# A planner's instruction orders and engine choices replaced in a fused attention and channel-mix kernel

## The chip, the cores and the metric

The kernel runs on one core of a Trainium2 chip. Times are microseconds (us) on the device; lower is better. The kernel before has a median of 170.34 us over 13 runs (169.53 to 171.25). The engines are PE (TensorE), VectorE (DVE in the profile), ScalarE (ACT), GpSimd (POOL) and SyncE (SP), which here only issues DMAs.

## What is computed

Attention with a sink of 4 keys and a window of 128, in 4 batches of 8 heads with 768 positions of 64 elements, and behind it a channel mix with a token shift:

```python
scores = np.where(is_sink | in_window, scale * q @ k.T, -1e9)
a = exp(scores - max); a = a / sum(a)
x = (a @ v).transpose(0, 2, 1, 3).reshape(B, S, H * D)      # [4, 768, 512]
xk = mu_k * x + (1 - mu_k) * x_prev                          # x_prev: x of the token before
xr = mu_r * x + (1 - mu_r) * x_prev
k = np.maximum(xk @ w_k, 0)                                  # w_k 512 x 1024
out = sigmoid(xr @ w_r) * ((k * k) @ w_v)                    # w_r 512 x 512, w_v 1024 x 512
```

All inputs and the output are float32; the kernel multiplies in bf16.

## The kernel before

The sequence is cut into 12 tiles of 256 tokens (u = 0 to 11: three for each of four batches; T = u % 3). For each tile:

- `load`: q, k and v of the tile, each 512 KB, go from HBM to the buffers `qs`, `ks`, `vs` (three of each), in one DMA or in two halves of 256 KB, all of them on SP's queue.
- `prepare`: casts to bf16 (`kb`, `qb`, `vb`), then a transpose to `kt` and `qt`. For k of tiles 4 to 11 and q of tiles 8 to 11 the transpose is a DMA on SP's queue (L608); for the others it is done on PE (`prep`, L621) and copied out of PSUM (L629).
- `attend`: scores `sc` for two pairs of heads at a time (L706), exp to `e` (L742, ScalarE), the mask (L756, VectorE), the product with v in `o` (L768 and L780), reciprocal and scaling to `x` (L793, L796).
- `mix`: transpose of x on PE (`xtp`, L819), copy to `xt` (L828), the token shift: `td` (L846) and four `xk` and four `xr` (L857).
- `ffn`: `kp` = xk @ w_k (L907), relu to `rl` (L917, L921), square to `kk` (L930, L934), `rp` = xr @ w_r (L946), tanh to `th` (L952), `vp` = kk @ w_v (L964), the gate in `ob` (L973; three `ob` buffers), and the store to HBM on SP's queue (L980).

The weights come as five loads of 1 MB (`wk` in two, `wr`, `wv` in two) and are cast once.

Every one of these steps is recorded as a numbered operation by `P.op` of the class `Plan`; the number is the place in the order of recording. `CHOICE` maps a number to an engine for operations that more than one engine can do. `ORDER` holds, for each engine, the numbers in the order in which it runs them. `Plan.schedule` merges the five lists into one program: it takes, again and again, the head of the list that its own model of durations lets start first, gives it the buffers of a pool that come free first by that model, and, where PE would be idle by that model in the first 32 us, puts in fills (L984: products with a tile of zeros, into a free bank). Constants of that model are the `service` of a DMA and the additions to the landing time in `schedule`. They are used for nothing else than the merge, the buffers and the number of fills. Each engine takes its instructions in order; an instruction that waits holds those behind it.

Numbers that are spoken of later: 0 to 66 are the loads. Of tile 7's, 8's, 9's, 10's, 11's loads: k is 38/39, 43/44, 49/50, 55/56, 61/62; q is 40, 45/46, 51/52, 57/58, 63/64; v is 41/42, 47/48, 53/54, 59/60, 65/66. The DMA transposes of tile 9 are 729, 731, 733, 735, of tile 10 806 to 812 (even), of tile 11 882 to 888 (even). The first scores of tiles 2, 9, 10 and 11 are 236, 783, 859 and 935. Stores: 470 and 466 of tile 3 (their `ob` is 469 and 465), 551 and 547 of tile 4, 627 and 623 of tile 5 (626, 622), 699 and 703 of tile 6 (698, 702).

Of the kernel before, what the change touches and what calls it, by code (L numbers as in the profile page):

```python
# [18 lines left out]
    83: "ACT", 87: "ACT", 89: "ACT", 93: "DVE", 96: "DVE", 97: "POOL", 99: "DVE", 102:  # L19
    "DVE", 103: "ACT", 104: "ACT", 128: "DVE", 134: "DVE", 137: "DVE", 140: "DVE", 141:  # L20
    "DVE", 150: "DVE", 178: "DVE", 181: "DVE", 187: "DVE", 190: "ACT", 191: "DVE", 200:
    "DVE", 208: "DVE", 209: "ACT", 261: "DVE", 270: "DVE", 271: "DVE", 276: "DVE", 300:
    "ACT", 341: "DVE", 344: "DVE", 346: "DVE", 350: "ACT", 352: "DVE", 359: "DVE", 368:
    "ACT", 372: "ACT", 376: "ACT", 417: "DVE", 421: "DVE", 427: "ACT", 428: "DVE", 437:
    "DVE", 446: "ACT", 454: "ACT", 458: "ACT", 495: "POOL", 499: "DVE", 500: "DVE", 502:
    "DVE", 505: "DVE", 506: "ACT", 511: "DVE", 518: "DVE", 527: "ACT", 531: "ACT", 535:
    "ACT", 539: "ACT", 574: "DVE", 579: "DVE", 581: "POOL", 584: "ACT", 585: "ACT", 607:
    "ACT", 656: "DVE", 660: "DVE", 661: "ACT", 663: "DVE", 670: "DVE", 679: "ACT", 683:
    "ACT", 691: "ACT", 734: "POOL", 736: "ACT", 737: "DVE", 742: "DVE", 749: "DVE", 758:
    "ACT", 761: "DVE", 766: "ACT", 770: "ACT", 813: "ACT", 814: "ACT", 823: "DVE", 832:  # L30
    "ACT", 839: "DVE", 840: "ACT", 844: "ACT", 883: "DVE", 885: "POOL", 889: "ACT", 890:
    "DVE", 899: "DVE", 908: "ACT", 912: "ACT", 915: "DVE", 920: "ACT", 958: "DVE", 974:
    "ACT", 982: "ACT", 1010: "ACT", 1014: "ACT",
# [24 lines left out]
        92, 95, 108, 109, 101, 79, 98, 118, 119, 115, 106, 111, 125, 121, 132, 158, 142,  # L58
        149, 129, 138, 135, 159, 156, 182, 188, 168, 169, 206, 234, 207, 161, 165, 175,
        171, 210, 192, 211, 199, 218, 219, 214, 179, 215, 185, 236, 289, 297, 301, 293,  # L60
        290, 298, 302, 294, 247, 239, 222, 224, 244, 250, 305, 230, 226, 255, 275, 227,
        259, 282, 231, 265, 309, 262, 310, 268, 317, 365, 307, 366, 342, 313, 328, 347,
        314, 373, 320, 374, 369, 325, 370, 336, 395, 377, 331, 351, 378, 383, 358, 381,
        393, 406, 385, 420, 386, 451, 273, 443, 452, 444, 389, 398, 425, 473, 403, 409,
        414, 390, 429, 447, 455, 436, 448, 456, 461, 471, 484, 459, 467, 498, 524, 536,
        525, 537, 503, 468, 528, 476, 529, 487, 552, 492, 508, 532, 481, 533, 463, 577,
        517, 510, 464, 563, 542, 555, 548, 540, 560, 549, 582, 630, 600, 586, 608, 601,
        566, 609, 544, 604, 571, 545, 605, 612, 593, 613, 641, 628, 616, 618, 633, 676,
        638, 677, 688, 680, 689, 681, 662, 704, 706, 649, 644, 684, 624, 685, 669, 620,
        625, 692, 621, 717, 709, 714, 694, 759, 755, 760, 756, 700, 741, 763, 739, 764,  # L70
        701, 767, 696, 725, 697, 768, 720, 783, 771, 773, 748, 779, 791, 775, 786, 780,
        794, 776, 815, 829, 837, 830, 833, 838, 834, 841, 857, 859, 802, 845, 797, 842,
        849, 822, 870, 853, 847, 862, 854, 905, 867, 906, 850, 909, 891, 910, 917, 913,
        878, 918, 923, 873, 921, 914, 935, 898, 929, 925, 933, 946, 930, 971, 979, 972,
        975, 980, 976, 938, 926, 954, 949, 943, 987, 983, 957, 984, 964, 989, 995, 991,
        996, 992, 999, 1003, 1000, 1004, 1007, 1011, 1008, 1012, 1019, 1015, 1017, 1020,
# [3 lines left out]
        69, 93, 96, 70, 102, 99, 80, 112, 113, 107, 116, 126, 137, 127, 122, 117, 123,  # L80
        128, 134, 150, 144, 147, 181, 145, 151, 152, 187, 146, 155, 153, 82, 81, 154, 148,
        140, 141, 208, 162, 163, 166, 176, 167, 172, 177, 173, 84, 194, 200, 195, 178,
        201, 196, 203, 202, 197, 221, 204, 85, 238, 213, 243, 191, 86, 217, 198, 240, 205,
        241, 249, 88, 245, 251, 246, 292, 252, 254, 90, 304, 256, 276, 257, 296, 277, 228,
        278, 261, 280, 284, 279, 285, 286, 232, 311, 341, 287, 344, 346, 319, 324, 281,
        270, 288, 271, 315, 335, 321, 326, 322, 330, 337, 327, 338, 417, 332, 352, 333,
        353, 397, 359, 354, 360, 356, 380, 361, 355, 362, 421, 387, 274, 364, 402, 413,
        399, 408, 400, 357, 404, 410, 405, 415, 411, 416, 391, 363, 431, 437, 434, 438,
        432, 450, 500, 439, 440, 433, 502, 442, 480, 499, 428, 486, 475, 491, 469, 477,
        478, 488, 505, 489, 435, 493, 509, 482, 494, 483, 574, 554, 441, 579, 511, 518,  # L90
        512, 559, 513, 519, 465, 556, 514, 557, 520, 561, 521, 562, 515, 565, 550, 523,
        632, 567, 516, 570, 522, 588, 568, 572, 573, 589, 637, 546, 590, 595, 591, 596,
        597, 656, 599, 634, 603, 635, 639, 643, 640, 611, 648, 663, 615, 592, 650, 645,
        651, 646, 660, 664, 665, 670, 598, 671, 708, 672, 626, 713, 666, 673, 710, 711,
        622, 715, 719, 716, 667, 724, 761, 687, 668, 742, 740, 743, 744, 746, 674, 675,
        726, 727, 702, 721, 722, 698, 762, 745, 737, 790, 749, 785, 750, 754, 792, 752,
        787, 747, 788, 751, 793, 781, 777, 801, 817, 818, 753, 839, 796, 836, 819, 803,
        804, 798, 820, 799, 821, 883, 823, 824, 861, 866, 826, 825, 863, 864, 855, 827,
        868, 877, 869, 851, 828, 893, 872, 879, 880, 894, 895, 874, 875, 896, 915, 899,
        900, 916, 904, 942, 901, 902, 937, 931, 948, 890, 897, 903, 953, 939, 940, 927,  # L100
        955, 950, 956, 944, 945, 951, 958, 978, 959, 962, 960, 986, 966, 963, 961, 967,
        968, 993, 997, 969, 970, 1002, 1006, 1021, 1029, 1025,
    ),
    "ACT": (
        67, 68, 91, 94, 100, 110, 114, 103, 104, 120, 124, 131, 133, 143, 130, 136, 139,
        160, 164, 183, 189, 157, 170, 174, 235, 209, 193, 83, 212, 184, 220, 180, 216,
        186, 237, 242, 190, 291, 299, 303, 248, 295, 223, 87, 253, 306, 225, 89, 258, 300,
        264, 260, 283, 267, 266, 263, 339, 269, 323, 318, 308, 367, 343, 334, 348, 329,
        375, 376, 371, 368, 396, 401, 372, 379, 419, 382, 394, 422, 384, 424, 412, 407,
        350, 445, 453, 426, 446, 474, 479, 430, 454, 427, 449, 457, 472, 462, 497, 460,  # L110
        485, 458, 490, 526, 538, 504, 530, 527, 553, 576, 558, 534, 531, 578, 535, 506,
        539, 543, 569, 564, 652, 541, 583, 631, 587, 602, 610, 654, 636, 658, 584, 606,
        594, 614, 585, 629, 617, 642, 619, 647, 678, 690, 705, 682, 607, 679, 707, 683,
        712, 691, 661, 728, 686, 730, 693, 718, 723, 732, 695, 757, 736, 765, 807, 766,
        758, 805, 769, 789, 772, 784, 774, 770, 811, 809, 795, 800, 816, 831, 835, 832,
        858, 860, 865, 846, 813, 843, 814, 840, 844, 848, 881, 876, 871, 907, 887, 892,
        911, 919, 912, 924, 908, 920, 941, 936, 889, 934, 922, 947, 952, 973, 977, 981,
        974, 982, 988, 985, 965, 990, 1001, 1005, 1009, 1013, 1014, 1010, 1016, 1018,
    ),
    "POOL": (  # L120
        73, 71, 78, 72, 76, 97, 75, 74, 77, 105, 272, 349, 495, 507, 581, 734, 738, 885,
    ),
    "SP": (
        0, 1, 3, 2, 4, 5, 7, 6, 16, 8, 10, 11, 9, 15, 12, 17, 18, 13, 14, 19, 20, 23, 25,
        24, 21, 22, 229, 340, 345, 28, 30, 29, 26, 233, 27, 418, 423, 312, 33, 31, 34, 35,
        392, 32, 496, 501, 36, 40, 38, 39, 37, 316, 575, 43, 580, 470, 45, 46, 388, 41,
        42, 44, 653, 655, 47, 659, 657, 49, 48, 551, 547, 51, 52, 53, 50, 731, 57, 735,
        729, 55, 627, 733, 623, 54, 466, 58, 56, 808, 699, 806, 812, 810, 63, 59, 60, 61,
        62, 782, 778, 64, 884, 882, 856, 886, 888, 703, 65, 66, 852, 932, 998, 928, 994,
        1022, 1030, 1026,  # L130
    ),
}


class Plan:

# [27 lines left out]
    def schedule(self):  # L164
# [37 lines left out]
        clock, port, dma, flying, mode = dict(BEGIN), {}, 0.0, [], 0  # L202
# [834 lines left out]
```

## Time and profile before

| | |
|---|---|
| median of 13 runs | 170.34 us (169.53 to 171.25) |
| the profiled execution, own time | 170.34 us |
| its span | 167.9 us |
| granted TensorE clock | 1.00 |
| HBM read, written | 24.12 MB, 6.29 MB |
| DMA packets | 81,762, of them 63,688 under 512 B |
| 256 KB load of k, v, q, from issue to landing (median) | 4.6, 4.6, 4.2 us |
| 1 MB load of a weight | 9.0 us |
| DMA transpose of k, q | 2.7, 3.2 us |
| store of 256 KB | 3.6 us |

The profile covers one execution. A group's row gives line, engine, operation, tiles, the count, then the engine's busy time and the mean of one, then the engine's idle time just before and what ended it. The chain of waits follows the work that ended last back to the start: each piece has its start, its length, and what it was.

### The profile page before, as it was taken

The page shows a single profiled execution, that of the slowest core. Times are in us where ns is not written, and L with a number is a line of the kernel's source. Part 1 is how long each engine was busy: PE and PEld are TensorE (multiplying, and loading weights), DVE is VectorE, ACT ScalarE, POOL GpSimd, SP SyncE. Part 2 cuts the span into 40 slices and gives each one's busy share as a digit, 9 for nine tenths or more (in the row PEclk, how much of TensorE's full clock was granted, in tenths as well). Part 3 has the DMA queues.
Part 4 walks back from the last instruction along what each step waited for, and adds up shares of the span by engine and source line. Part 5 has one row for each costly group of instructions (what it writes and reads, how often), then busy time and mean ns, then how long its engine had stood idle before and what let it go on. Part 6 is the DMA issues. An engine that isn't in the chain of part 4 may idle for free.

```text
span 167.9 us, 4234 instructions
## 1 busy us (share of the span) xinstructions
PE 160.8 (96%) x1627; PEld 105.0 (63%) x1627; DVE 145.0 (86%) x378; ACT 136.2 (81%) x223; POOL 12.7 (8%) x41
## 2 busy tenths in 40 slices
PE   7988999999999999999999999999989999999991
PEld 2445477855567586676576875766565685774850
DVE  2759999998999999999999889989988998988611
ACT  3777969999999999889899999768758978863450
POOL 7630000000100200100000001010000100000000
PEclk9999999999999999999999999999999999999999
DMA  4999999999879899997796797969979959100403
GB/s 138 246 294 331 206 359 301 282 358 274 198 179 270 188 215 257 158 265 164 188 275 137 166 290 173 158 162 264 202 77 234 286 129 246 67 4 0 168 19 125
DMA packets 81762, 33.81 MB, mean 201 GB/s; under 512 B 63688, under 2 KB 76240, under 8 KB 81744
## 3 DMA queue, kind: packets, MB, share of 16 engines
q1 hardware_dynamic: 81728, 33.56, 83.0%
q8 instruction: 12, 0.20, 0.5%
q14 instruction: 6, 0.05, 0.1%
q10 hardware_dynamic: 16, 0.00, 0.0%
HBM read 24.12 MB, written 6.29 MB: 181 GB/s over the span
## 4 chain that ended last, share of the span: by engine, by line
PE 65%; DVE 17%; DMA 12%; ACT 2%; issue 2%; SPq 0%
PE bank L907 17%; PE bank L964 15%; PE bank L946 9%; DMA qs<-in_q_dram 7%; PE sc L706 5%; PE bank L780 5%; PE bank L984 4%; DVE xk L857 3%; DMA kt<-kb 3%; DVE ob L973 2%; PE bank L621 2%; DVE x L796 2%; PE bank L819 2%; DMA out_dram<-ob 2%; PE bank L768 2%
## 5 line engine op out<-in xcount | busy, mean ns | idle before, releaser
L907 PE MATMUL bank<-xk,wk_sb 128*128 128x256 bf16 x384 | 50.2, 273 | 0.2 <-DVE wk_sb L563 0.2
L964 PE MATMUL bank<-wv_h,kk 128*128 128x512 bf16 x184 | 46.3, 379 | 0.0
L742 ACT ACTIVATE e<-sc 128x1024 bf16<-128x1024 f32 (+1 forms) x48 | 44.3, 964 | 1.7 <-PE sc L706 1.5
L907 PEld LDWEIGHTS <-wk_sb 128*128 128x128 bf16 x384 | 35.6, 98 | 8.5 <-DVE wk_sb L563 0.4
L917 ACT ACTIVATE rl<-bank 128x512 bf16<-128x512 f32 x44 | 25.9, 613 | 11.9 <-PE bank L907 10.0
L964 PEld LDWEIGHTS <-kk 128*128 128x128 bf16 x184 | 16.5, 98 | 14.3 <-DVE x L796 0.3
L756 DVE TENSOR_TENSOR e<-e,mask 128x1024 bf16<-128x1024 bf16 (+1 forms) x40 | 25.2, 641 | 0.1
L946 PE MATMUL bank<-wr_sb,xr 128*128 128x512 bf16 x96 | 24.0, 379 | 0.0
L857 DVE SCALAR_TENSOR_TENSOR xr<-td,mu_all,xt 128x256 bf16<-128x256 bf16 x48 | 22.7, 481 | 0.1
L857 DVE SCALAR_TENSOR_TENSOR xk<-td,mu_all,xt 128x256 bf16<-128x256 bf16 x48 | 22.0, 484 | 0.1
L973 DVE SCALAR_TENSOR_TENSOR ob<-th,bank 128x512 f32<-128x512 f32 x23 | 15.4, 681 | 5.7 <-PE bank L964 4.9
L796 DVE TENSOR_TENSOR x<-bank,rec 128x256 bf16<-128x256 f32 x48 | 19.3, 413 | 0.4
L780 PE MATMUL bank<-vb,e 128*128 128x65 bf16 x352 | 19.3, 193 | 0.4 <-DVE x L796 0.3
L780 PEld LDWEIGHTS <-e 128*128 128x128 bf16 x352 | 17.0, 97 | 3.5 <-issue 0.4
L934 ACT ACTIVATE kk<-rl 128x512 bf16<-128x512 bf16 x29 | 17.7, 632 | 0.4 <-DVE rl L921 0.3
L952 ACT ACTIVATE th<-bank 128x512 f32<-128x512 f32 x24 | 14.4, 603 | 2.2 <-PE bank L946 2.1
L706 PE MATMUL sc<-qt,kt 64*128 64x128 bf16 (+1 forms) x256 | 14.1, 238 | 0.8 <-DMA kt<-kb 0.7
L946 PEld LDWEIGHTS <-xr 128*128 128x128 bf16 x96 | 8.6, 98 | 8.4 <-issue 0.5
L793 DVE RECIPROCAL rec<-bank 128x4 f32<-128x4 f32 x48 | 8.3, 177 | 6.1 <-PE bank L780 5.3
L706 PEld LDWEIGHTS <-kt 64*128 64x128 bf16 x256 | 8.9, 94 | 6.9 <-issue 2.8
L768 PE MATMUL bank<-vsink,es 128*128 128x130 bf16 x64 | 12.4, 221 | 0.0
L984 PE MATMUL bank<-warm 128*128 128x512 bf16 x30 | 10.3, 448 | 1.1 <-DVE warm L1000 1.1
(75 smaller groups left out, 172.0 us busy)
## 6 DMA issues: line engine op xcount, KB each, us to landing
vs<-in_v_dram SPq DMA_DIRECT2D x24, 256.0 KB, 4.6
out_dram<-ob SPq DMA_DIRECT2D x23, 256.0 KB, 3.6
ks<-in_k_dram SPq DMA_DIRECT2D x18, 256.0 KB, 4.6
qs<-in_q_dram SPq DMA_DIRECT2D x7, 512.0 KB, 6.5
qs<-in_q_dram SPq DMA_DIRECT2D x10, 256.0 KB, 4.2
w<-in_moe_w_k_dram SPq DMA_DIRECT2D x2, 1024.0 KB, 9.0
w<-in_moe_w_v_dram SPq DMA_DIRECT2D x2, 1024.0 KB, 9.0
ks<-in_k_dram SPq DMA_DIRECT2D x3, 512.0 KB, 7.3
```

The costliest lines, as they stand in the source:

```text
L706: nc.tensor.matmul(out=sc[:, a, o0:o1], lhsT=lhs[rows], rhs=rhs[rows], start=u not in BIAS, stop=True, skip_group_check=u in BIAS)
L742: nc.scalar.activation(out=buf[ek][:, :, lo:], in_=buf[sck][:, :, lo:], func=AF.Exp, scale=scale)
L756: nc.vector.tensor_tensor(out=at, in0=at, in1=m, op=ALU.mult)
L780: nc.tensor.matmul(out=o[:, g, a, :], lhsT=e[:, a, e0:e0 + 128], rhs=rhs, start=(T == 0 and i == 0), stop=(i == len(blocks) - 1), skip_gro ...
L796: P.op("DVE", dve(256), lambda ok=ok, rk=rk, c=c: nc.vector.tensor_tensor(out=buf["x", u][:, :, 128 * c:128 * c + 128].rearrange("p g (a d ...
L857: nc.vector.scalar_tensor_tensor(out=buf[key][:, c0 + i, :], in0=buf[tk][:, i, :], scalar=mu[w][:, c0 + i:c0 + i + 1], in1=xt[:, c0 + i, t ...
L907: nc.tensor.matmul(out=ps[:, i, :], lhsT=wk_sb[:, c, 128 * f:128 * f + 128], rhs=xk[:, c, :], start=(c == 0), stop=(c == NC - 1), skip_gro ...
L917: nc.scalar.activation(out=buf[rk], in_=buf[psk].rearrange("p (i t) -> p i t", i=2), func=AF.Relu)
L934: nc.scalar.activation(out=buf["kk", u][:, 2 * f2:2 * f2 + 2, :], in_=buf[rk], func=AF.Square)
L946: nc.tensor.matmul(out=buf[psk], lhsT=buf["xr", u][:, c, 128 * g:128 * g + 128], rhs=wr_sb[:, c, :], start=(c == 0), stop=(c == NC - 1))
L964: nc.tensor.matmul(out=buf[psk], rhs=wv_h[:, f, :], lhsT=buf["kk", u][:, f, 128 * g:128 * g + 128], start=(f == 0), stop=(f == NF - 1))
L973: P.op("DVE", dve(512), lambda psk=psk, tk=tk, bk=bk: nc.vector.scalar_tensor_tensor(out=buf[bk], in0=buf[tk], scalar=1.0, in1=buf[psk], o ...
```

## The change

All five lists of `ORDER` and the table `CHOICE` are replaced, and the constants of the planner's model that are shown below. The arithmetic, the tiles, the pools and the emitted instructions of an operation stay as they are. 90 operations change engine (casts, copies out of PSUM, relus and squares); the number of fills goes from 30 to 14.

The constants:

```diff
-                    end += (300.0 if dma < 4700.0 else 900.0 if dma < 16800.0 else
-                            1500.0 if dma < 32000.0 else 700.0 if dma < 37000.0 else 150.0)
+                    end += (300.0 if dma < 4700.0 else 400.0 if dma < 16800.0 else
+                            600.0 if dma < 37000.0 else 150.0)
...
-                        service=1330.0, descs=1024, take=[] if g else [("vs", key)],
+                        service=1300.0, descs=1024, take=[] if g else [("vs", key)],
...
-                service=128 * (h1 - h0) * 1.96 + 45.0, descs=128 * (h1 - h0), take=[] if h0 else [(name + "s", key)],
+                service=128 * (h1 - h0) * 1.745 + 45.0, descs=128 * (h1 - h0), take=[] if h0 else [(name + "s", key)],
...
-             service=3050.0, descs=660, take=[("w32", key)], writes=[(name + "32", i)])
+             service=2850.0, descs=660, take=[("w32", key)], writes=[(name + "32", i)])
```

SP's and POOL's lists:

```diff
     "POOL": (
-        73, 71, 78, 72, 76, 97, 75, 74, 77, 105, 272, 349, 495, 507, 581, 734, 738, 885,
+        73, 71, 72, 75, 78, 76, 77, 74, 105, 82, 344, 272, 419, 422, 427, 507, 506, 737,
+        738, 883,
     ),
     "SP": (
-        0, 1, 3, 2, 4, 5, 7, 6, 16, 8, 10, 11, 9, 15, 12, 17, 18, 13, 14, 19, 20, 23, 25,
-        24, 21, 22, 229, 340, 345, 28, 30, 29, 26, 233, 27, 418, 423, 312, 33, 31, 34, 35,
-        392, 32, 496, 501, 36, 40, 38, 39, 37, 316, 575, 43, 580, 470, 45, 46, 388, 41,
-        42, 44, 653, 655, 47, 659, 657, 49, 48, 551, 547, 51, 52, 53, 50, 731, 57, 735,
-        729, 55, 627, 733, 623, 54, 466, 58, 56, 808, 699, 806, 812, 810, 63, 59, 60, 61,
-        62, 782, 778, 64, 884, 882, 856, 886, 888, 703, 65, 66, 852, 932, 998, 928, 994,
+        1, 0, 2, 3, 4, 5, 7, 6, 16, 10, 11, 8, 9, 15, 12, 17, 18, 13, 14, 20, 19, 23, 25,
+        24, 21, 229, 22, 340, 345, 30, 28, 29, 26, 233, 27, 33, 312, 418, 423, 31, 34, 35,
+        496, 32, 392, 501, 36, 37, 38, 388, 316, 40, 39, 45, 575, 43, 44, 580, 41, 466,
+        46, 42, 47, 653, 655, 49, 657, 659, 51, 53, 50, 48, 470, 547, 52, 551, 54, 731,
+        55, 729, 733, 735, 57, 627, 58, 56, 61, 62, 703, 699, 63, 808, 806, 810, 812, 64,
+        782, 59, 60, 623, 884, 882, 886, 778, 65, 888, 66, 856, 852, 932, 998, 928, 994,
         1022, 1030, 1026,
```

PE's list, its start and the stretch from tile 8's to tile 11's scores (each line as it stands, others left out):

```diff
-        92, 95, 108, 109, 101, 79, 98, 118, 119, 115, 106, 111, 125, 121, 132, 158, 142,
-        149, 129, 138, 135, 159, 156, 182, 188, 168, 169, 206, 234, 207, 161, 165, 175,
-        171, 210, 192, 211, 199, 218, 219, 214, 179, 215, 185, 236, 289, 297, 301, 293,
...
-        701, 767, 696, 725, 697, 768, 720, 783, 771, 773, 748, 779, 791, 775, 786, 780,
-        794, 776, 815, 829, 837, 830, 833, 838, 834, 841, 857, 859, 802, 845, 797, 842,
-        849, 822, 870, 853, 847, 862, 854, 905, 867, 906, 850, 909, 891, 910, 917, 913,
-        878, 918, 923, 873, 921, 914, 935, 898, 929, 925, 933, 946, 930, 971, 979, 972,
...
+        95, 92, 79, 108, 109, 101, 98, 118, 106, 119, 111, 115, 121, 125, 142, 132, 129,
+        158, 138, 159, 149, 182, 156, 188, 135, 168, 169, 165, 234, 161, 175, 206, 171,
+        207, 192, 210, 199, 211, 218, 214, 179, 215, 219, 185, 236, 297, 301, 289, 302,
...
+        725, 696, 701, 739, 783, 697, 748, 767, 771, 768, 773, 786, 791, 794, 779, 775,
+        780, 829, 776, 830, 837, 802, 815, 838, 833, 847, 834, 797, 845, 841, 822, 842,
+        857, 859, 849, 853, 909, 905, 870, 906, 854, 850, 910, 862, 867, 917, 923, 918,
+        913, 878, 891, 914, 935, 873, 921, 929, 898, 925, 933, 946, 930, 926, 971, 979,
...
```

ScalarE's list between the scores of tile 1 and those of tile 2, to show what the start looks like (139, 160, 164 and 183 to 189 are copies and exps of tiles 1 and 2; 208 and 209 relu and square of tile 0; 83 a cast of wk; 141 a cast of v):

```diff
-        67, 68, 91, 94, 100, 110, 114, 103, 104, 120, 124, 131, 133, 143, 130, 136, 139,
-        160, 164, 183, 189, 157, 170, 174, 235, 209, 193, 83, 212, 184, 220, 180, 216,
-        186, 237, 242, 190, 291, 299, 303, 248, 295, 223, 87, 253, 306, 225, 89, 258, 300,
+        139, 160, 164, 157, 136, 141, 189, 174, 235, 170, 208, 83, 209, 212, 184, 180,
+        216, 220, 186, 237, 242, 291, 299, 213, 303, 248, 295, 253, 223, 225, 217, 306,
```

## The prediction

> **What bounds the kernel now.** I read the page first, then stages of the span, then the chain of waits, then the order of SP's queue. Part 1 of the page and the DMA row of part 2:
>
> ```profile
> span 167.9 us, 4234 instructions
> PE 160.8 (96%) x1627; PEld 105.0 (63%) x1627; DVE 145.0 (86%) x378; ACT 136.2 (81%) x223; POOL 12.7 (8%) x41
> ...
> DMA  4999999999879899997796797969979959100403
> ```
>
> PE looks like the only bound, but the DMA row is also at 7 to 9 tenths until slice 33 (about 139 us). The table of stages (instructions of each engine, granted clock, DMA share, GB/s) tells the same in numbers:
>
> ```profile
> core 0: us, PE busy (x) PEld busy (x) DVE busy (x) ACT busy (x) POOL busy (x), PEclk, DMA share, GB/s
> 0.00:30.00 30.00, 27.42 (x280) 16.37 (x281) 23.34 (x70) 22.59 (x35) 7.23 (x30) 1.00 0.99 264
> 30.00:70.00 40.00, 39.94 (x422) 26.15 (x420) 38.24 (x100) 38.84 (x65) 2.36 (x5) 1.00 0.99 243
> 70.00:104.00 34.00, 34.00 (x370) 23.31 (x369) 32.55 (x85) 31.73 (x55) 1.60 (x4) 1.00 0.90 206
> 104.00:140.00 36.00, 35.28 (x360) 23.36 (x355) 32.76 (x83) 28.55 (x48) 1.51 (x4) 1.00 0.92 189
> 140.00:168.00 28.00, 24.13 (x212) 15.82 (x206) 18.09 (x44) 14.45 (x24) 0.00 (x0) 1.00 0.26 84
> ```
>
> From 30 us on PE has hardly a gap, and the DMA engines are 90 to 99% taken until 140 us. So there are two bounds that run side by side: PE's work, and the transfers that must land ahead of it. Where they touch, the chain of waits shows it (start, us, what):
>
> ```profile
> 110.08 3.47 DMA out_dram<-ob
> 113.58 0.69 DVE ob L973
> ...
> 121.09 4.21 DMA kt<-kb
> 125.35 0.51 PE sc L706 x10
> ```
>
> A store had to land before VectorE could refill its `ob` buffer, and a transpose had to land before the scores of tile 10. The second is PE's only clear gap after the start. In the order of time on PE:
>
> ```profile
> 125.35 0.51 PE L706 MATMUL sc<-qt,kt 64*128 64x128 bf16 x10 [0.72 <-DMA kt<-kb]
> ```
>
> The start is different: fills (the group below) and waits for casts.
>
> ```profile
> L984 PE MATMUL bank<-warm 128*128 128x512 bf16 x30 | 10.3, 448 | 1.1 <-DVE warm L1000 1.1
> ```
>
> **What PE needs.** The work on PE is the same before and after but for the fills. From start to start on the trace (kp 0.44 us, vp and rp 0.86, o 0.35 or 0.18, sc 0.55 or 0.44, prep and xtp 0.22, and so on, times their counts) it is about 145.3 us. PE runs from 0.8 to 163.2 us, so about 17 us are lost: about 14 before 30 us (fills, waits), some 3 afterwards. That is all that an order can win back.
>
> **Part 1: 16 fills fewer** (30 to 14). At 0.22 us warm they are 3.5 us of PE, but each stands where PE waited anyway. What releases PE at 20 to 28 us is the k of tile 2: it lands near 25 us, is cast (0.42), transposed (0.39), copied out on ScalarE (0.74), then sc(2,0) starts at 27.9; and xk of tile 1 from VectorE at 28.0. I walked both queues of the new order with the durations of the rows. VectorE's part comes to xk(1) at about 27.2 (0.8 earlier: it has less ahead of it). ScalarE's part is longer by about 0.4: it takes over kb(1,0), kb(1,1), vb(1,1), rl(0,0) (3 x 0.51 + 0.48) and hands over xt(0), qt(2,0), xt(1) (0.48 + 0.58 + 0.48), and it waits for rl(0,0) behind o(1,2). So e(2,0) starts 0.4 later and the kp of tile 1 earlier; rp(0) comes out between 0.4 earlier and 0.4 later. I take 0. The first score is the same kind of wash: q is loaded first, its two copies move from VectorE to ScalarE, 6.5 us for 6.4.
>
> Here the clock has a rule against the change. Row first: granted clock 1.00 in every stage, with PE 8.88 of 10 us busy at 10 to 20 us, fills included. The Trainium skill (TensorE: Matmul & The Clock Gate, section on HAM oscillation) says that idle gaps of about 3.4 us halve the clock. Without fills PE would be busy some 6 of those 10 us, but in pieces: the longest gap of my walk is under 2 us (from 12.4 to 14.3, waiting for k of tile 1). By the row the cost is 0; by the rule, if one window still counted as idle, half of 3.4 us, 1.7. I take 0 and keep 1.7 for the range.
>
> **Part 2: engines of 90 casts, copies, relus and squares.** With the mean of each kind VectorE loses about 0.9 us of 145 and ScalarE 1.3 of 136; two more casts go to POOL (8 for 6, 0.6 to 1.0 us each, and wk(1) about 1.2 to 2.0 as twice the size). POOL is 8% busy and PE reaches wk(1) near 22.5, after 20.2 + 2.0. Cost 0; at worst one late kp, 0.4. After 30 us VectorE's queue in the new order asks for about 2 us less work ahead of the same PE work: cover, not gain, as PE has no gaps there to close except the 0.72.
>
> **Part 3: weights behind v of tile 1.** The bytes up to the second half of wk are the same, so it lands at 23.1 as before; wk's first half lands about 1.5 later (20.2 for 18.8), v(1) about 2.5 earlier. PE does o(1) before kp(0) accordingly. In the walk above; 0 more.
>
> **Part 4: SP's order against PE's order from 95 us on.** This decides. One load of 256 KB costs 256 KB / 206 GB/s = 1.27 us in the third stage and 1.39 in the fourth; I use 1.33. Here the skill would say otherwise: DMA: Bandwidth & Descriptors, Specifications, gives about 358 GB/s from HBM for a core, 0.73 us a load, and DMA would not bind. But it also asks for pieces of at least 512 B, and this trace has 63,688 of 81,762 packets below that; the row decides. By the rule the sums below would be about half.
>
> Count what SP issues before the last transposes of a tile, and what PE does before its scores:
> - sc(9,0), number 783 (last transposes 733 before, 735 after): the same number of loads and of stores in both orders, but PE comes to it 1.7 us sooner (vp 697 and kp 767 and 768, 0.86 + 2 x 0.44, moved behind it). Before, the transpose issued at 110.71 landed (median 2.7) near 113.4 to 113.7, and PE took it at 113.99: slack about 0.4. Late by 1.3.
> - sc(10,0), 859 (810 before, 812 after): three loads more ahead of its transposes (61, 62, 63: both k and one q of tile 11): 4.0 us; PE comes 2.7 later. 1.3 tighter, at the place which already waits 0.72.
> - sc(11,0), 935 (888 in both): one load more (65, v of tile 11): 1.33; PE comes 1.2 sooner (rp 921 and o 873, 0.86 + 0.35, moved behind). 2.5 tighter. Before:
>
> ```profile
> 134.30 1.23 SPq L608 DMA_TRANSPOSE kt<-kb  x1
> 135.62 2.12 SPq L608 DMA_TRANSPOSE qt<-qb  x1
> ...
> 139.62 0.62 PE L706 MATMUL sc<-qt,kt 64*128 64x256 bf16 x12
> ```
>
> The last one, plus a median 3.2 to land, is there at 138.8 at the latest: slack 0.7. Late by 1.8.
> - ob: the buffer for tile 6's output 698 is freed by store 627 in the new order (623 before), which has one load more ahead of it, at the same PE work: +1.33 on the 113.58 piece of the chain above. And output 622 hangs on store 470, which SP now reaches three loads later; that takes what slack it had.
>
> These delays don't add: waiting at sc(9) makes sc(10) less late. What counts is the largest, 1.8, against a stage in which DMA is 8 to 10% free (some 3 us of 36). SP waits less where v(9), k(11), q(11) are fetched early, and part of that can come back. Between 0 and 1.8 I take 1.2, nearer the upper end, because the early loads fill just those gaps with work that isn't urgent. What is late is the transposes of one of tiles 9 to 11 and all PE work behind them (23.6 us behind sc(11,0)).
>
> **Part 5: the tail.** After 146 us the same kp, vp, rp in another order; kk(11,2) has about 0.5 us of cover from vp and rp. 0.
>
> **Sum.** Its own execution took 170.34 us, 167.9 of span and 2.4 around it; the median of the runs shown is 170.34 too. 170.34 + 0 + 0 + 0 + 1.2 + 0 = **171.5 us**. PE's gain at the start, if any, would be lost here too, since the transfers don't come sooner.
>
> **Rivals.**
> - *Faster, 169.2.* The early gain of 0.4 stays and the 0.72 at sc(10,0) goes, as PE meets it 2.7 us later. For it: the waits of SP (24.2 us in five waits for `ob`, some 20 for casts before transposes) leave room for a better order; VectorE gets 2 us of cover. Against: sc(9) and sc(11) have the tighter count. 170.34 - 0.4 - 0.7 = 169.2.
> - *No difference, 170.3.* The free DMA time swallows part 4, and ScalarE swallows part 1.
> - *Slower, further.* A wait in the start breaks the clock (1.7) on top of part 4, or the `ob` wait holds VectorE's casts, so that SP's transposes start later and the delay of 1.3 comes once in each of two tiles: 170.34 + 1.2 + 1.5 = 173.0. It decides from the point where the DMA share in 104 to 140 us falls under 0.9 and PE shows gaps above 2 us.
>
> **How the numbers follow.** Forecast 0.50, faster rival 0.27, no difference 0.13, further slower 0.10. Measured against no change, 0.3% is about 0.5 us. Of the forecast 0.46 lies beyond that and 0.04 within; of the faster rival 0.25 beyond; no difference splits 0.03, 0.07, 0.03. Faster 0.28, same 0.13, slower 0.59. The range takes in 169.2 and 173.0; the forecast's own is 170.5 to 172.3.
>
> **What would show it.** Right: PE gaps released by DMA kt or qt before the scores of tiles 9 and 11 of 1 us or more, and a longer `ob` wait near 113 us. The start: rp(0) at 33 us, clock 1.00, as many useful matmuls by 30 us. Wrong: no DMA-released gap after 90 us (then SP had more slack than I counted), or tile 2's scores a microsecond or more earlier together with an earlier end.

## The result, and the profile after

The kernel after takes 167.65 us (median of 11 runs, 166.85 to 169.65) against 169.91 us (48 runs) for the kernel before: a ratio of 0.987, 95% interval 0.9844 to 0.9895. The forecast was 171.5 us, slower; the kernel became 2.3 us faster. The profiled execution has a span of 166.0 us for 167.9. Here and below, ratios and intervals leave out executions more than 1.5% above the fastest of their kernel, and medians in us take in all.

The head of the page and its DMA row, for the kernel after:

```profile
span 166.0 us, 4208 instructions
...
PE 157.9 (95%) x1611; PEld 104.7 (63%) x1611; DVE 144.8 (87%) x378; ACT 133.9 (81%) x221; POOL 16.0 (10%) x43
...
DMA  4999999999979979999996899779959792100403
```

The stages of the kernel after (columns as in the prediction's table):

```profile
0.00:30.00 30.00, 25.58 (x271) 16.31 (x272) 22.68 (x70) 23.99 (x37) 8.53 (x30) 1.00 1.01 267
30.00:70.00 40.00, 40.00 (x423) 26.45 (x421) 38.69 (x99) 39.27 (x67) 5.01 (x8) 1.00 1.03 246
70.00:104.00 34.00, 33.90 (x372) 23.39 (x370) 32.57 (x86) 32.12 (x54) 0.61 (x1) 1.00 1.02 223
104.00:140.00 36.00, 36.00 (x360) 23.62 (x359) 32.48 (x84) 27.02 (x47) 1.84 (x4) 1.00 0.81 189
140.00:166.00 26.00, 22.39 (x195) 14.89 (x193) 18.43 (x44) 11.47 (x21) 0.00 (x0) 1.00 0.16 61
```

Two stages differ from before. In 70 to 104 us the DMA engines moved 223 GB/s for 206: 17 GB/s over 34 us is 0.58 MB, or 2.2 loads of 256 KB. In 104 to 140 us their share is 0.81 for 0.92, and PE has no idle time. The chain of waits of the kernel after, in the stretch in which before's had a store and a transpose (start, us, what):

```profile
126.07 0.25 PE bank L684 x4
126.32 0.55 PE sc L707 x12
126.87 1.83 PE bank L965 x8
...
136.29 0.44 PE bank L908 x4
136.73 0.55 PE sc L707 x12
```

These are the scores of tiles 10 and 11. From 111 us to the last gate every piece of the chain is PE's own work; no DMA stands in it. The last transpose of tile 9 lands at 110.8 us (before 114.0) and of tile 11 at 136.0 (138.9). A transpose reports its landing in 16 parts; of the last one of tile 10, 15 parts are there at 123.9 us, but the 16th comes at 125.9 (before 125.3), just ahead of PE's scores at 126.3. So tile 10's transposes came no sooner; PE asked for them later. SP issues the first and the last of tile 9's last four transposes (731 and the last) as follows, in the kernel before and then in the kernel after:

```profile
103.83 1.20 SPq L608 DMA_TRANSPOSE qt<-qb  x1
...
110.71 1.22 SPq L608 DMA_TRANSPOSE kt<-kb  x1
```

```profile
102.35 1.20 SPq L609 DMA_TRANSPOSE qt<-qb  x1
...
106.89 1.22 SPq L609 DMA_TRANSPOSE qt<-qb  x1
```

How late PE is at a point can be read apart from the order: take the start of a score and subtract the PE work that the list puts ahead of it, fills left out. The work is counted with the median time from start to start of each kind of operation in the two traces, 147.5 us in all. I call the rest PE's **loss**. It is 13.10 us before and 12.29 after at the first scores of tile 2 (236), and 16.48 and 14.74 at the last product of tile 11. So 0.8 us comes from the first 28 us and 0.9 us from what lies behind them. In between the two are even, with 2.2 and 2.1 us from 236 to the first scores of tile 10 (859). The 0.9 us falls inside those scores: it is the wait of 0.72 us that the prediction shows, and it is gone.

That wait does not belong to the old lists alone, however. Five runs below keep them behind 236 (e1, e2, e4, e6, e11, with 7 to 28 fills or other constants), and in none of their profiled executions does PE have it: from 859 to 935, the first scores of tile 11, the loss grows by 0.2 to 0.5 us, for 1.1 in the kernel before.

### The profile page after: what moved, and what is told of

Same layout as the page of the kernel before. It is cut to its first block, busy times and chain, and to the rows that moved or that the text cites. A ratio compares the mean times of both kernels' runs of the same rounds, so it can differ in the third digit from the quotient of the medians.

```text
span 166.0 us, 4208 instructions
## 1 busy us (share of the span) xinstructions
PE 157.9 (95%) x1611; PEld 104.7 (63%) x1611; DVE 144.8 (87%) x378; ACT 133.9 (81%) x221; POOL 16.0 (10%) x43
## 4 chain that ended last, share of the span: by engine, by line
PE 80%; SPq 8%; DMA 6%; DVE 2%; issue 1%
PE bank L965 24%; PE bank L908 23%; PE bank L947 13%; DMA ks<-in_k_dram 6%; PE sc L707 6%; PE bank L781 6%; SPq L409 3%; SPq L392 3%; PE bank L820 3%; PE bank L769 2%; PE bank L622 2%; SPq L427 1%; PE bank L878 1%; PE bank L684 1%; DVE e L757 1%
## 5 line engine op out<-in xcount | busy, mean ns | idle before, releaser
L908 PE MATMUL bank<-xk,wk_sb 128*128 128x256 bf16 x384 | 50.8, 273 | 0.7 <-DVE wk_sb L564 0.7
L743 ACT ACTIVATE e<-sc 128x1024 bf16<-128x1024 f32 (+1 forms) x48 | 45.4, 973 | 5.4 <-PE sc L707 5.4
L965 PE MATMUL bank<-wv_h,kk 128*128 128x512 bf16 x184 | 45.7, 379 | 0.0
L935 ACT ACTIVATE kk<-rl 128x512 bf16<-128x512 bf16 x32 | 20.4, 641 | 0.1
L781 PEld LDWEIGHTS <-e 128*128 128x128 bf16 x352 | 16.4, 97 | 3.0 <-ACT e L743 0.9
L794 DVE RECIPROCAL rec<-bank 128x4 f32<-128x4 f32 x48 | 7.7, 174 | 3.1 <-PE bank L781 2.7
L847 DVE TENSOR_TENSOR td<-xt 128x512 bf16<-128x512 bf16 x24 | 10.1, 422 | 0.2
```

What stands on the lines that cost most here:

```text
L743: nc.scalar.activation(out=buf[ek][:, :, lo:], in_=buf[sck][:, :, lo:], func=AF.Exp, scale=scale)
L781: nc.tensor.matmul(out=o[:, g, a, :], lhsT=e[:, a, e0:e0 + 128], rhs=rhs, start=(T == 0 and i == 0), stop=(i == len(blocks) - 1), skip_gro ...
L908: nc.tensor.matmul(out=ps[:, i, :], lhsT=wk_sb[:, c, 128 * f:128 * f + 128], rhs=xk[:, c, :], start=(c == 0), stop=(c == NC - 1), skip_gro ...
L935: nc.scalar.activation(out=buf["kk", u][:, 2 * f2:2 * f2 + 2, :], in_=buf[rk], func=AF.Square)
L965: nc.tensor.matmul(out=buf[psk], rhs=wv_h[:, f, :], lhsT=buf["kk", u][:, f, 128 * g:128 * g + 128], start=(f == 0), stop=(f == NF - 1))
```

## The experiments

Ratios are to the kernel before in the same set of runs, with 95% intervals. Each set ran on a chip of its own, and the median of before moved between 169.4 and 169.9 us from set to set, so kernels of one set are compared in us where that is possible; a loss or a landing is of one profiled execution. Every experiment leaves the arithmetic whole.

**Fills.** The rule that puts them in has an end time in the planner's own clock; this leaves those of its first 4.6 us, which are eight with the old start's lists and seven with the new (the expectations below say 8 for both). It is tried in the kernel before (e4) and in the kernel after (e9):

```diff
-    P.fill_until = 32000.0
+    P.fill_until = 4600.0
```

> The kernel before with the first 8 fills alone (8 for 30). If fills hold up ready work: faster by 0.3 to 0.8 us, sc(2,0) sooner. If they stand where PE waits: no difference, clock 1.00. If the gaps let the clock gate close: clock under 1.00 before 30 us and 1 to 2 us slower.

> The kernel after with only the 8 fills of the first 4.6 us (14 before this edit); orders, engines and constants as after. Theory (a fill often stands ahead of work that is already ready, so each late fill costs a part of its 0.22 to 0.45 us): 0.3 to 0.6 us faster than after, a ratio to before of 0.983 to 0.986, with the first scores of tile 2 at 27.0 for 27.4 us. Rival A (the six fills left sit in real gaps): as after, 0.987. Rival B (PE's clock falls without them): granted clock under 0.98 in 0 to 30 us and a ratio of 0.99 or more.

The other direction, in the kernel after (e12), gives 35 fills for 14 with every list unchanged:

```diff
-                while t - now > (300.0 if now > 4000.0 else 600.0) and now < self.fill_until:
+                while t - now > (60.0 if now > 4000.0 else 600.0) and now < self.fill_until:
```

> The kernel after with more fills at the start, 35 for 14, and nothing else changed: the planner puts one wherever its model sees 0.06 us of idle PE after 4 us, for 0.30. Theory (fills stand ahead of ready work): 0.6 to 1.2 us slower than after, a ratio to before of 0.990 to 0.994, and the scores of tile 2 start 0.6 to 1.2 us later than after's 27.4. Rival (fills only take time in which PE waits anyway, as the prediction held): 0.987, scores of tile 2 at 27.4.

And the new constants alone in the kernel before (e6), which change the fills to 21, the merge and the buffers:

> The kernel before with the new constants alone: order and engines as before, 21 fills for 30 and other buffers. If fills held up ready work at the start: up to 0.5 us faster at sc(2,0). If a fill stands only where PE waits anyway, as I forecast: no difference (within 0.3 us).

Measured: e4 168.70 us, 0.9959 (0.9933 to 0.9984); e6 167.79 us, 0.9936 (0.9907 to 0.9966); e9 167.76 us, 0.9909 (0.9882 to 0.9936); e12 169.51 us, 0.9999 (0.9965 to 1.0032). So 22 fills fewer are worth about 0.7 us with before's order (0.41% of 169.4), and 28 more cost 1.75 us in the new one (e12 less e9, one set). Seven or 14 make no difference that can be told: 167.76 and 167.65 us in two sets, 167.56 (e18, below, with one load moved as well) and 167.48 (e17) in one.

e6 gains more than either of its expectations, with not one list changed: 1.1 us by its ratio, 1.6 by the medians of its set (167.79 for 169.39). Worked through `Plan.schedule`, it differs from the kernel before in nine fills and in the PSUM bank of 154 buffers out of 628, and in nothing else. All edits of the fills move banks as well (160 in e4, 101 in e9, 192 in e12), so the gain of fewer fills is that of fills and banks together; neither was tried without the other.

What a fill can hold up is seen on PE in order of time. The kernel before, from the last transposes of tile 1's k on:

```profile
15.26 0.38 PE L621 MATMUL bank<-ident,kb 128*128 128x128 bf16 x4
15.47 0.59 PE L984 MATMUL bank<-warm 128*128 128x512 bf16 x2
16.00 0.61 PE L706 MATMUL sc<-qt,kt 64*128 64x256 bf16 x12
16.55 0.82 PE L984 MATMUL bank<-warm 128*128 128x512 bf16 x3
17.30 0.29 PE L683 MATMUL bank<-qt,ksink 128*32 128x256 bf16 x4
17.53 0.40 PE L621 MATMUL bank<-ident,qb 128*128 128x128 bf16 x4
17.76 0.38 PE L984 MATMUL bank<-warm 128*128 128x512 bf16 x1
18.19 0.40 PE L621 MATMUL bank<-ident,qb 128*128 128x128 bf16 x4
18.42 0.59 PE L984 MATMUL bank<-warm 128*128 128x512 bf16 x2
18.85 1.03 PE L713 MATMUL sc<-ob,ident 128*128 128x512 bf16 x4
19.81 0.39 PE L706 MATMUL sc<-qt,kt 64*128 64x256 bf16 x6
```

The same stretch of the kernel after:

```profile
14.95 0.62 PE L707 MATMUL sc<-qt,kt 64*128 64x256 bf16 x12
15.49 0.40 PE L820 MATMUL bank<-ident,x 128*128 128x128 bf16 x4
15.73 0.39 PE L622 MATMUL bank<-ident,qb 128*128 128x128 bf16 x4
16.05 0.29 PE L684 MATMUL bank<-qt,ksink 128*32 128x256 bf16 x4
16.27 0.40 PE L622 MATMUL bank<-ident,qb 128*128 128x128 bf16 x4
17.01 0.38 PE L622 MATMUL bank<-ident,kb 128*128 128x128 bf16 x4 [0.34 <-DVE qt L630]
17.23 1.03 PE L714 MATMUL sc<-ob,ident 128*128 128x512 bf16 x4
18.56 0.61 PE L707 MATMUL sc<-qt,kt 64*128 64x256 bf16 x12 [0.31 <-ACT kt L630]
```

In the kernel before not one row here shows a wait: eight fills (about 1.8 us at 0.22) take the place of the waits. In the kernel after PE does a transpose of x and one of k more between the first and the second pair of scores, waits 0.65 us for data, and still needs 3.6 us for 3.8. With before's own start the second pair begins at 18.7 us in e4 (8 fills) and at 20.0 in e5 (below: 30 fills), although k of tile 1 landed at 13.0 us in e4 and at 12.8 in e5. A fill stands in PE's order at a place where a model expected a wait; where the data come sooner it stands ahead of ready work. The granted clock of the profiled executions is 0.995 or more with 7, 8, 14, 30 and 35 fills. In e12:

```profile
L985 PE MATMUL bank<-warm 128*128 128x512 bf16 x35 | 12.8, 445 | 1.3 <-DVE warm L1001 1.1
```

```profile
138.10 0.62 PE L707 MATMUL sc<-qt,kt 64*128 64x256 bf16 x12 [1.07 <-DMA qt<-qb]
```

The first row is the group of fills, the second PE at tile 11. The sign that was expected did not come: tile 2's scores start at 27.7 us for 27.4, not 0.6 us later or more. The loss is only 0.25 us larger at 236 (12.54 for 12.29) and 0.3 at tile 9, but then the transpose of tile 11 lands at 138.1 for 136.0 and PE waits 1.07. SP's list and all buffers but PSUM banks are the same as in the kernel after. So most of e12's cost is seen there and not at the fills; how they lead to it is not shown. It is the wait that part 4 of the prediction forecast for the kernel after, and it was not there with 14 fills: the late part runs close to its edge.

**Start or late part.** Each half of the lists and engine choices with the other half of the other kernel, cut at number 236: new start alone with its 14 fills (e2), new late part alone with before's 30 fills (e3), then both with the fills cut to 7 and 8 (e11, e10). The new constants went with the new start: e2, e9 and e11 have them, e3, e4 and e10 have the old.

> The new order and choices up to the first scores of tile 2 (236), the old ones behind. If the gain has two halves (start 0.8 us, wait at tile 10 0.9 us): 0.8 us faster than before if the lead is kept to the end, with the DMA-released gap at tile 10's scores still there or larger. If the transfers set the end, as I forecast: the lead is lost by tile 10 and the time is that of before. If the late order alone brought the gain: no difference.

> The old order up to 236, the new one behind. Two halves: 1.0 us faster (no gap above 0.3 us at the scores of tiles 9 to 11), start as before, sc(2,0) at 28.2. If the early lead alone brought it: no difference or slower, with a gap of about 1 us at tiles 9 or 11, since the transfers would come 0.8 us later than in the changed kernel.

> The old start and the new order from tile 2's scores on, with 8 fills only. Against the same old start with the old late order and 8 fills (measured 0.996), it tells what the late order alone is worth. Theory (the late order fetches three to four loads earlier, and this pays only where the start hands over earlier and the transfers run ahead): no gain over it, 0.994 to 0.998, and PE waits 1.5 to 2.3 us for the transposes of tile 11. Rival (the late order is worth its part by itself, and the first test of it was spoiled by 30 fills): 0.987 to 0.991, no wait above 0.8 us at tiles 9 to 11.

> The new start with the old order from tile 2's scores on, with 8 fills only (14 before this edit, measured 0.9955). With the three other corners (old and old 0.996, old and new, new and new, all with 8 fills) it tells whether start and late part add. Theory (start worth 0.5 to 0.8 us, late part pays only with it): 0.992 to 0.995. Rival (all of the start's gain is its fewer fills): 0.996, the same as the old start with 8 fills.

e2 took 168.46 us, 0.9955 (0.9931 to 0.9978), and e3 169.67 us, 0.9987 (0.9951 to 1.0022). Alone they explain less than the whole. With the fills cut:

| fills | median, ratio | loss at 236 | loss at the last product |
|---|---|---|---|
| 8; old start, old late (e4) | 168.70, 0.9959 | 12.83 | 15.82 |
| 7; new start and constants, old late (e11) | 168.92, 0.9969 | 12.32 | 15.49 |
| 8; old start, new late (e10) | 167.71, 0.9908 | 12.04 | 14.59 |
| 7; new start and constants, new late (e9) | 167.76, 0.9909 | 12.27 | 14.43 |

The lower three are of one set. The start's order, with the constants, is worth nothing (167.76 for 167.71), though in e2 it looked like 0.9 us; e4 and e6 have as much or more with the old start, from fewer fills and other banks. The late part is worth 1.2 us in this set (168.92 to 167.76) and needs no new start; with 30 fills it did not show (e3). My own theory for e10, that the late order pays only with the new start, fell. Its size depends on what it is held against: e6, all old lists with 21 fills and the new constants, has 0.9936 for 0.9908 and 0.9909, only 0.3% more, with intervals that overlap.

Where the 1.2 us falls is not one place. Between e11 and e9 the loss differs by 1.06 us at the end. By the first scores of tile 3, at 43 us, e11's has grown by 1.0 us since 236 and e9's by 0.2; from 38 to 41 us PE in e11 has a late start at each of the two transposes of tile 3's k. Another 0.3 us comes at tile 11's first scores. Between e4 and e10 that 0.3 us is there again, but the rest is not at tile 3, and 0.8 us of it is there at 236 already, where both have the same lists.

The stage of 70 to 104 us goes with the late part. e11 first, then e9:

```profile
70.00:104.00 34.00, 34.00 (x378) 23.34 (x376) 32.54 (x85) 31.86 (x56) 2.15 (x4) 1.00 0.94 210
104.00:140.00 36.00, 35.76 (x357) 23.65 (x354) 33.01 (x83) 28.57 (x48) 1.10 (x3) 1.00 0.91 190
```

```profile
70.00:104.00 34.00, 34.00 (x375) 23.73 (x373) 32.97 (x88) 32.51 (x56) 0.61 (x1) 1.00 1.03 219
104.00:140.00 36.00, 36.00 (x360) 23.50 (x358) 32.52 (x84) 27.03 (x46) 1.84 (x4) 1.00 0.80 187
```

With the same start and fills the new late part moves 9 GB/s more before 104 us. The last transpose of tile 11 lands at 135.5 for 138.6.

**SP at the start.** v of tile 1 ahead of the first half of wk, in the kernel before with the new constants (e1); and wk ahead again in the kernel after (e7):

```diff
-        0, 1, 3, 2, 4, 5, 7, 6, 16, 8, 10, 11, 9, 15, 12, 17, 18, 13, 14, 19, 20, 23, 25,
+        0, 1, 3, 2, 4, 5, 7, 6, 16, 10, 11, 8, 9, 15, 12, 17, 18, 13, 14, 19, 20, 23, 25,
```

> The constants of e6 and v of tile 1 ahead of wk's first half on SP, nothing else (28 fills). If the 1 MB load right behind them holds up q and k of tile 1: k(1) lands near 12.9 us instead of 14.1, and sc(1,0) starts about 1 us sooner than in e6. If the landing is set by the bytes in front alone, as in my walk: k(1) at 14.1 as before. The end: no more than 0.3 us faster, since kp(0) then waits for wk in an order that wants it first; or slower by as much.

> The changed kernel with wk's first half ahead of v of tile 1 on SP again (the place it had before; 21 fills). If the landing of q(1), k(1) makes the early lead: k(1) lands 1.2 us later, sc(1,0) and sc(1,2) 1 us later, and with v(1) late too the time rises by 1 us or more over the changed kernel. If the lead comes from VectorE's and ScalarE's lists: sc(2,0) stays near 27.4.

e1: 170.36 us, 1.0060 (1.0027 to 1.0092). e7: 169.96 us, 1.0027 (0.9995 to 1.0059). Each is slower than the kernel that it was made from (e6 at 0.9936, after at 0.987). PE's first product with wk in e1, then in e7:

```profile
22.31 0.61 PE L907 MATMUL bank<-xk,wk_sb 128*128 128x256 bf16 x4 [1.25 <-DVE wk_sb L563]
```

```profile
24.07 0.61 PE L908 MATMUL bank<-xk,wk_sb 128*128 128x256 bf16 x4 [0.96 <-DVE wk_sb L564]
```

It stands at 20.6 us in the kernel before, with no wait, and at 21.8 in the kernel after, behind a wait of 0.72 us. So the product comes 1.7 and 2.3 us later than in the kernels with the orders that belong together, and PE's loss at 236 is 14.64 in e1 for 12.75 in e6, and 14.28 in e7 for 12.29. The edit also changes the number of fills (28 in e1, 21 in e7), so a part of the difference may be theirs. k of tile 1, which landed at 14.1 us in before's profile and 12.8 in after's, lands at 12.8 in e1 and e7 alike: wk's place does not set it.

**The place of tile 10's scores on PE.** In the kernel before, two numbers moved later, about as far as in the kernel after, and nothing else (e5):

```diff
-        834, 841, 857, 859, 802, 845, 797, 842, 849, 822,
+        834, 841, 845, 842, 802, 797, 849, 857, 859, 822,
```

> The kernel before with the first scores of tile 10 (857, 859) behind 845, 842, 802, 797 and 849 on PE (about 2.9 us later), nothing else. If PE's order made the wait: the gap of 0.72 us goes and the time falls by 0.7 to 0.9 us. If the transfers set the end: tile 11's scores wait instead and the time stays.

170.91 us, 1.0099 (1.0061 to 1.0137), slower than either expectation. The wait for the transpose is gone, but others stand in its place: around tile 10's scores, from 126 to 130 us, PE waits 0.55 us for VectorE's x and 1.09 for ScalarE's e. The loss grows by 0.9 us from tile 9's scores to tile 10's and by 1.9 more to tile 11's, whose last transpose lands at 140.9. Asking later for what is late did not help; what depends on these scores came later too, SP's transposes among it.

**Loads on SP, later or more.** Two useless 256 KB loads into spare tiles ahead of the second half of v of tile 9, in the kernel after (e8):

```diff
+        if (u, g) == (9, 1):
+            for t in spare:
+                nc.sync.dma_start(out=t, in_=v[b, :, s0:s0 + 128, :].rearrange("h p d -> p h d"))
```

> The changed kernel with two useless loads of 256 KB into spare tiles just ahead of v(9)'s second half on SP. If transfers go at a fixed rate of 1.33 us each and set the end (my part 4): tile 9's last transpose lands 2.7 us later, its scores wait 2 us, the time is 2 us longer than the changed kernel's. If SP waits there for a cast anyway and the engines have room: transposes of tile 9 within 0.5 us of 110.8, the time within 0.3 us of the changed kernel's.

168.98 us, 0.9961 (0.9932 to 0.9991): 1.3 us over the kernel after's median from another set, 0.67 us for each load (1.5 us by the ratios). Neither expectation came: the last transpose of tile 9 lands at 111.9 us for 110.8, 1.1 us later for two loads where 1.33 us each make 2.7. PE in e8 at tile 9:

```profile
112.00 0.51 PE L714 MATMUL sc<-qt,kt 64*128 64x256 bf16 x8 [0.54 <-DMA qt<-qb]
```

So transfers do bind here as soon as there are two more; at this place the kernel after has less than that to spare. Then the two groups of early loads that the prediction had priced were put back, 61 to 63 behind 812 (e15) and 65 behind 888 (e16), in the kernel after:

```diff
-        56, 61, 62, 703, 699, 63, 808, 806, 810, 812, 64,
+        56, 703, 699, 808, 806, 810, 812, 61, 62, 63, 64,
...
-        884, 882, 886, 778, 65, 888, 66,
+        884, 882, 886, 778, 888, 65, 66,
```

> The kernel after with the loads of k (both halves) and of the first half of q of tile 11 (61, 62, 63) moved back behind the last transpose of tile 10 (812) on SP, where they stood before. By the prediction's count they cost the transposes of tile 10 4.0 us, so these land at 120 to 121.5 for 123.9. Theory P (they delay what is urgent): as fast as after or up to 0.5 us faster, 0.984 to 0.987, since PE does not wait there. Theory G (they fill time in which SP would wait for casts and stores, and their own transposes of tile 11 need them early): tile 10's transposes land less than 2 us earlier, tile 11's at least 1.5 us later than 136.0, PE waits for them, 0.991 to 0.998.

> The kernel after with the load of the first half of v of tile 11 (65) behind the last transpose of tile 11 (888), as before, in place of ahead of it. By the prediction's count 888 lands 1.3 us sooner (134.7 for 136.0). Since PE did not wait for it in the kernel after, the time should be as after, 0.985 to 0.988. If 888 lands at 136 all the same, the load cost nothing there.

e15 took 175.29 us, 1.0351 (1.0315 to 1.0387); e16 167.48 us, 0.9917 (0.9883 to 0.9951). In e15 the transposes of tile 10 do land sooner, at 121.5 us for 125.9 (123.9 without the straggling part). But ScalarE shows who needed the loads:

```profile
123.87 0.62 ACT L594 CAST kb<-ks 128x512 bf16<-128x512 f32 x1 [6.34 <-DMA ks<-in_k_dram]
124.39 0.80 ACT L744 ACTIVATE e<-sc 128x768 bf16<-128x768 f32 x1
```

and PE:

```profile
125.85 0.51 PE L782 MATMUL bank<-vb,e 128*128 128x65 bf16 x6 [5.01 <-DVE e L758]
```

The cast of tile 11's k stands in ScalarE's new list ahead of exps that PE is waiting for. The load is late, the cast waits 6.34 us, the exp waits behind it, PE stands 5.01 us. I had expected at most 1% and the wait at tile 11's transposes; it came sooner and was larger. Behind it the clock fell, which no shorter gap of PE did (the page's slices are 4.3 us here, so the empty one is 121.4 to 125.7 us):

```profile
PE   7977899999999999999999999998099999999991
PEclk9999999999999999999999999999858999999998
```

Of the 7.6 us over the kernel after, 5.0 are the wait; of the rest about 2 us are work at the lower clock, an estimate from the loss, which grows by 8.2 us between tile 9's and tile 10's scores for 0.2 in the kernel after.

In e16 SP issues 888 earlier (first the kernel after, then e16; start, us on SP's queue):

```profile
131.45 0.53 SPq L981 DMA_DIRECT2D out_dram<-ob  x1
132.03 0.42 SPq L392 DMA_DIRECT2D vs<-in_v_dram  x1
132.55 1.35 SPq L609 DMA_TRANSPOSE qt<-qb  x1
```

```profile
130.31 0.53 SPq L982 DMA_DIRECT2D out_dram<-ob  x1
130.93 1.23 SPq L610 DMA_TRANSPOSE qt<-qb  x1
```

It lands at 133.4 for 136.0. Of these 2.6 us 1.1 are there already in the transpose before it (131.4 for 132.6 us) and 1.5 are the load's, beside the 1.33 that the prediction counted. The time is unchanged, since PE did not wait there.

**SP's list against the other lists.** New late part with 8 fills but SP's list of before (e13); all as before with 8 fills but SP's new list from the cut on (e14).

> Old start, 8 fills, the new late part on PE, VectorE, ScalarE and GpSimd, but SP's list as before throughout. With the new SP list this measured 0.9908, with everything old 0.9959. Theory S (SP's own list carries the late gain): 0.995 to 1.000, and PE waits 1 us or more for a transpose of tile 9, 10 or 11. Theory E (the engines' orders carry it, by casting and freeing buffers sooner for SP and by asking for the transposes at better places): 0.989 to 0.992.

> The opposite: everything old with 8 fills (0.9959), but SP's late list the new one. Theory S: 0.989 to 0.992. Theory E: 0.996 or above, since SP's new list is met by casts and buffers that come in the old order; if it clashes with them, above 1.000.

e13: 189.66 us, 1.1176 (1.1135 to 1.1217). e14: 177.33 us, 1.0451 (1.0408 to 1.0494). Neither theory's number came; either change alone is far slower than neither. In e13 ScalarE's casts wait 10.9 us for loads of k, the longest 8.9, and PE 7.5 us for one masked e, as in e15. So the late gain belongs to the lists together, and cannot be shared out between SP and the engines.

**Once more, and a try for better.** The kernel after again (e17), and with 7 fills and 65 behind 888 (e18):

> The kernel after, unchanged, once more. If the first ratio holds: 0.985 to 0.989. If the ratio moves by some 0.3% from one set of runs to the next: 0.989 to 0.992, as the kernels with the new late part and 8 fills gave, with a median of 167.5 to 167.9 us either way.

> The kernel after with 8 fills for 14 and with the load 65 behind the transpose 888 on SP. Theory (after has neither a fill nor a load on its bound any more): within 0.2% of the kernel after in the same call. Rival (the two margins add): 0.3% or more faster than it, 167.2 us or less.

e17: 167.48 us, 0.9869 (0.9838 to 0.9900); e18: 167.56 us, 0.9881 (0.9846 to 0.9915). The ratio of 0.987 holds; the 0.991 of e9, e10 and e16 came with a lower median of before in those sets. No version measured here is faster than the kernel after by more than can be told.

## Why the prediction was wrong, step by step

- **What bounds the kernel**: right in kind. More transfers cost time (e8), and so did more fills (e12), those mostly through one transfer that came late. But a DMA share of 90% was read as "8 to 10% free", with a fixed price for each load; that failed below.
- **Part 1, fills at 0**: wrong. The step "each stands where PE waited anyway" failed: 22 fills fewer gain about 0.7 us, the moved PSUM banks included. The clock, weighed there and taken at 0, was right: 1.00 in every stage with 14 fills. The walk's end, 0 from the start's order itself, came true with the fills cut (e10 and e9).
- **Part 2, engines at 0**: not tried alone, and e13 to e15 say that choices and lists cannot be judged apart.
- **Part 3, weights behind v at 0**: no cost is seen in the change as made, although PE waits 0.72 us for a cast of wk; one side of it without the other costs 1.2 to 1.6% (e1 against e6, e7 against after), fills included.
- **Part 4, +1.2**: the step that decided, and wrong in sign: with the fills cut the late part gives -1.2 in its set. What failed is the time axis under the count. The counts of loads were right. But landings and issue times were taken from before's trace and the new loads added to them, "late by 1.3" at tile 9 and "late by 1.8" at tile 11. In the kernel after no wait of PE behind 90 us ends with a DMA: tile 9's last transpose lands at 110.8 us for 114.0 and tile 11's at 136.0 for 138.9, sooner by about 3 where a delay was counted.
- The list with more loads ahead of a transpose had begun to issue them earlier. Transpose 731, the first of the last four of tile 9, has 55 loads and 10 stores ahead of it for 54 and 9, and SP still issues it at 102.35 us for 103.83. Between it and the last transpose the old list has two loads and a store and the new one a single load; the prediction counted only the totals ahead of the last, which are equal. So the last is issued at 106.9 us for 110.7: 1.5 us from the lead at 731 and 2.3 from this regrouping.
- The price of a load, 1.33 us, came near in one place only, 1.5 us for one load (e16). For the three of e15, counted at 4.0, it is 4.4 us against the kernel after with its straggling part and about 1.5 against e9 and e16, where tile 10's last transpose lands at 123. In e8 a load cost a transpose 0.55 us and the kernel about 0.67, nearer the 0.73 that the prediction worked out and set aside. "Work that isn't urgent" failed too: casts of the early loads stand ahead of tile 9's exps (e15).
- **Part 5, tail at 0**: right; from tile 11's first scores (935) to the last product the loss grows by 0.1 us in both.
- **Rivals**: the faster one (169.2) named the wait of 0.72 us that goes and an earlier start, and had both too small: its -1.1 us was -2.3. It missed the fills. Its reason, PE asking later for tile 10, is not enough (e5), and other runs with the old late lists lack the wait without it; to that extent it was lucky. The room that it saw in SP's waits for `ob` is largely not there: 20.7 of the 24.2 us lie behind 140 us, where only stores are left.
- **The size**: -0.7 for fewer fills and -1.2 for the late part make -1.9 of -2.3 us. This is one way of splitting, from two sets; e6, which gains 1.1 to 1.6 us with all lists old, overlaps with it and is not in it. About 0.4 us of the distance to the forecast is its base, 170.34 us for a measured 169.91. Three readings in the working were a little off and change nothing: PE's work is 147.5 us and not 145.3, PE's last product ends at 164.1 and not 163.2, and tile 2's scores start at 28.2 and not 27.9.

Two things stay open. The first is what gave SP its lead between 60 and 104 us: the lists could not be taken apart (e13, e14). The traces show one candidate. With the old late lists SP waits 1.9 to 2.9 us near 62 us, ahead of store 392, for VectorE to fill an `ob`; with the new ones, where 496 and 32 stand ahead of that store, at most 1.2. No run isolates this wait. The second is how far the gain of fewer fills is that of the PSUM banks that move with them.

## What to carry to other kernels

When a queue's order is replaced as a whole, do not hang its new entries on the old trace's times: rebuild the issue times from the first changed entry on, or bound the slack from both sides by a full load or two. Count what stands between the transposes, too, and not only the totals ahead of the last. An idle share of a tenth in DMA can hide two loads in 34 us. Fills, prefetches and casts in in-order lists need not be free at the place where a model puts them; test them alone before crediting an order with their gain.

## What the runs showed of the hardware

- Seven fills, all before 5 us, left the granted clock at 1.00 in e9, with PE busy 25.7 of the first 30 us; fewer were not tried. A wait of PE of 2.16 us (e14) left it at 1.00 too; behind one of 5.01 us (e15) a slice of 4.3 us has 5 tenths.
- The DMA share passes 1 (1.03 in the kernel after from 30 to 70 us, 1.13 in e10 from 70 to 104), so it is not a utilisation that ends at 1; the same engines moved 206 GB/s at a share of 0.90 and 223 at 1.02.
- SP's issue of one DMA transpose takes 1.2 us as a rule, but 2.51 us for 808 in the kernel before and 1.76 in the kernel after, each behind loads just issued, and 3.22 us for 496 in the kernel after. SP is issuing for 30.1 of the 34 us from 102 to 136 in the kernel before and 30.9 in the kernel after; whether that is a limit of its own was not tested.
- A transpose's landing can come in parts: 15 of 16 parts of tile 10's last one are there at 123.9 us in the kernel after, the 16th 2.0 us later.
